# Two pairs' keys times values as one run of products, in front of their queries; whole transposes for the second batch; a new order of the opening

## The chip, the cores and the metric

The kernel runs on one core of one Trainium2 chip. The metric is the device time of one execution in microseconds (us); the smaller, the better. Before the change it is 903.7 us, the median of three runs (903.17 to 904.11).

## What is computed

An attention without softmax, then a feed-forward block:

```python
kv  = np.einsum('bhsd,bhse->bhde', k, v)      # 8 batches, 8 heads, 576 tokens, 64 features
out = np.einsum('bhsd,bhde->bhse', q, kv)
rms = np.sqrt(np.mean(out * out, axis=-1, keepdims=True) + 1e-06)
x   = out / rms * g_norm                      # heads side by side: 4608 tokens x 512
g   = np.maximum(x @ w_in, 0.0) ** 2          # w_in 512 x 2048, w_out 2048 x 512
y   = g @ w_out
```

Everything is computed in float32. The weights arrive as 64-bit floats, so the kernel loads them as raw words and converts them itself.

## The kernel before, in words

**Heads come in pairs.** Four pairs (p = 0 to 3) hold the eight heads of a batch b. A pair's 576 tokens are four chunks of 128 tokens and 64 last tokens. The last tokens of an even batch lie in partitions 0 to 63 of k_rest, v_rest and q_rest, those of the odd batch after it in partitions 64 to 127.

**Keys times values** (key_value, L399 to L430) takes for each pair, chunk and head a product of 128 tokens by 64x64 features, and at the end of the pair, for each head, one over the 64 last tokens. Each float32 product is two instructions in the trace. The first kind uses half the columns of the array (128*64 in the profile), the second a quarter of it (64*64). ACT then copies the sums into kv_all (L418, L419). key_value is called for one pair at a time in batches 0 and 1 and for two pairs from batch 2 on.

**Queries are transposed** in transposed_query (L365 to L393): for batches 0 and 1 on TensorE, by a product with an identity (L388), one for each chunk and head, so 16 instructions a pair. For later batches VectorE does it (L371). The queries' last tokens of both first batches go through nc.tensor.transpose (L396), four for all four pairs, which are four instructions.

**Queries times kv** (products_x, L432 to L451) makes two tiles of tokens (a pair of ns) from 64 instructions in the same 64*64 form as the last tokens' products. query (L486) issues products_x, then key_value for the next batch if it was given keys, and then the squares; query_means (L493) is the same without keys and with the means. The rest of the normalising is on VectorE (DVE), with the root on ACT.

**The feed-forward** works in nine strips of 512 tokens. Its matrices are multiplied by Strassen's scheme: seven products for eight. Strip 0 computes the up half plainly (up_first, L749) and the down half with one level (down), strip 1 has one level up (up) and two down (down_deep), the later strips two levels in both (up_slot, down_deep). The second level's weights are sums that strip 0 and 1 make on DVE and POOL, store in DRAM (w_out, w_deep, w_in_deep) and stream back (w_blk).

**The opening** (L639 to L647) is a list of slices: act (ACT's two passes over a weight piece, L241 and L244), piece (its four DVE steps, L253 to L262), T (transposed_query), K (key_value), Q (first_queries, L522, with its squares and means), N (first_normalized, L531), F (first_features, L546) and U (first_up, L556, the products of strip 0's first weight columns). Every engine runs its share of a slice in the order of the list, and waits in that order.

**After the opening** attend(n) issues slices up to number n between the steps of the strips. In strip 0, step i runs up_first for i below n_up = 16 and down afterwards; the slices of batch 1 are spread by L1261 to L1263. In strip 1 they are spread evenly over 25 steps.

**The order of transfers** is SP's: nearly all DMAs are issued by SP in program order, and SP waits in front of each for what it needs. The pairs of batch 1 are loaded by load_next in steps 0 and 1 of strip 0, except pair 3, whose load (k, v, then q) is issued inside key_value of pair 0 (load_next at the end of key_value). Batch 1's q comes with one DMA a pair, in packets of 1 KB.

Of the kernel before, what the change touches and what calls it, by code (L numbers as in the profile page):

```python
# [10 lines left out]
FP32 = mybir.dt.float32  # L11
# [9 lines left out]
def kernel(  # L21
# [34 lines left out]
    nc = tc.nc  # L56
    P = 128
    B, H, S, D = q.shape
# [3 lines left out]
    NP = H // 2  # L62
    FC = d_ff // P
    C = S // P
    REST = S - C * P
# [37 lines left out]
    def load(b, p, q_eng, names="kvq", parts=range(4)):  # L103
        hs = slice(2 * p, 2 * p + 2)
        inputs = (("q", q, q_eng), ("k", k, nc.sync), ("v", v, nc.sync))
        if b == 0 and p >= 2:

            h_place = g_pool.tile([P, 4, C * P], FP32, name="first_qkv", tag="gt")
        if b == 1 and p == 2:
            h_place = spare_pool.tile([P, 3, C * P], FP32, name="more_qkv")  # L110
        placed = (b, p) in ((0, 2), (0, 3), (1, 2))
        for i, (n, src, eng) in enumerate(inputs if b == 0 else inputs[1:] + inputs[:1]):
            if n not in names:
                continue
            whole = src[b, hs, 0 : C * P].rearrange("h (sp c) d -> sp h c d", c=C)
            if n == "q" and b >= Q_ON_PE:

                t = qkv_pool.tile([P, 4 * C, SQ], FP32, name=n, tag=n, bufs=3) if 0 in parts else main[n, b, p]
                for a in parts:
                    h, f = divmod(a * SQ, D)  # L120
                    eng.dma_start(
                        out=t[ts(a, SQ)],
                        in_=src[b, 2 * p + h, 0 : C * P, f : f + SQ].rearrange("(k i) f -> i k f", k=4 * C),
                    )
            elif n != "q":
                if placed:
                    t = h_place[:, i].rearrange("p (h c d) -> p h c d", h=2, c=C)
                else:
                    t = qkv_pool.tile([P, 2, C, D], FP32, name=n, tag=n)
                eng.dma_start(out=t, in_=whole)  # L130
            else:

                if placed:
                    t = h_place[:, i].rearrange("p (h c d) -> p h c d", h=2, c=C)
                else:
                    t = qkv_pool.tile([P, 2, C, D], FP32, name=n, tag=n, bufs=3)
                eng.dma_start(out=t, in_=whole)
            main[n, b, p] = t


# [218 lines left out]
    def keep_busy(ps, n):  # L359


        for _ in range(n):
            nc.tensor.matmul(ps, lhsT=ident, rhs=ident[:, : ps.shape[1]], start=True, stop=True)

    def transposed_query(b, p):  # L365
        while any(f == load and a[:2] == (b, p) for f, a in drips):
            drip()
        t = main.pop(("q", b, p))
        if b >= Q_ON_PE:
            qT[b, p] = qt_pool.tile([P, C, P], FP32, name="qT", tag="qT")  # L370
            nc.vector.transpose(out=flat(qT[b, p]), in_=flat(t))  # L371
            if b % 2 and p == NP - 1:
                while any(f == load_q_rest and a[0] <= b for f, a in (*rest_drips, *drips)):
                    drip(not drips)
                nc.vector.transpose(
                    out=open_rest(b).rearrange("p q (k t) -> p q k t", k=4),
                    in_=squares(q_rest[b // 2]).rearrange("p k q f -> p q k f"),
                )
            drip_queries()
            if p == NP - 1 and b + 1 < B:  # L380
                (rest_drips, drips)[b % 2 == 0].extend((load_q_rest, (b + 1, nc.sync, a)) for a in range(4))
            return
        ps = apsum.tile([P, C, P], FP32, name="t_ps", tag="at")
        if (b, p) == (0, 0):
            keep_busy(ps[:, 0], 7)
        for c in range(C):
            for h in range(2):
                nc.tensor.matmul(ps[ts(h, D), c, :], lhsT=t[:, h, c], rhs=ident, start=True, stop=True)  # L388
        qT[b, p] = qt_pool.tile([P, C, P], FP32, name="qT", tag="qT")
        nc.scalar.copy(qT[b, p], ps)  # L390
        if (b, p) == (1, NP - 1):
            drip_queries()
# [6 lines left out]
    def key_value(b, *ps_of):  # L399
        while any(f == load and a[:2] == (b, p) or f == load_rest and a[0] == b for _, f, a in keys_due for p in ps_of):  # L400
            _, f, a = keys_due.popleft()
            f(*a)
        ps = apsum.tile([P, len(ps_of), D], FP32, name="kv_ps", tag="at")
        for i, p in enumerate(ps_of):
            tk, tv = main.pop(("k", b, p)), main.pop(("v", b, p))
            if (b, p) == (0, 0):
                keep_busy(ps[:, 0], 5)
                warm = apsum.tile([P, NT, P], FP32, name="x_ps", tag="first")[:, 0]
            half = slice(REST * (b % 2), REST * (b % 2 + 1))
            for c in range(C + 1):  # L410
                if (b, p, c) == (0, 0, C):
                    keep_busy(warm, 2)
                for h in range(2):
                    a, w = (t[:, h, c, :] if c < C else r[half, 2 * p + h] for t, r in ((tk, k_rest), (tv, v_rest)))
                    nc.tensor.matmul(ps[ts(h, D), i], lhsT=a, rhs=w, start=c == 0, stop=c == C)  # L415
        at = (NP * b + ps_of[0]) % (2 * NP)
        d = kv_all[:, at : at + len(ps_of)]
        nc.scalar.copy(d[0:D, :, 0:D], ps[0:D])  # L418
        nc.scalar.copy(d[D:P, :, D:P], ps[D:P])  # L419
        for i, p in enumerate(ps_of):  # L420
            kvd[b, p] = d[:, i]
            if b < 2:
                if b == 1 and p == 0:
                    load_next()
            else:
                u = next(to_load, None)
                if u is not None:
                    keys_later(load, *u, nc.sync, "kv")
                if p == NP - 1 and b + 1 < B:
                    keys_later(load_rest, b + 1, nc.sync)  # L430
# [30 lines left out]
    def mean_of(sqs):  # L461
        ms = small.tile([P, 2, H], FP32, name="ms", tag="ms")[:, : len(sqs)]
        for i, sq in enumerate(sqs):
            if len(sq.shape) == 3:
                sq = sq.rearrange("p r e -> p (r e)")
            nc.vector.reduce_sum(out=ms[:, i], in_=by_head(sq), axis=AX.X)
        nc.vector.tensor_scalar(out=ms, in0=ms, scalar1=1.0 / D, scalar2=EPS, op0=ALU.mult, op1=ALU.add)
        return ms
# [15 lines left out]
    queried = []  # L484

    def query(ns, *keys):  # L486
        ps = products_x(ns)
        if keys:
            key_value(*keys)
        parts = [ps[:, :, i] for i in range(len(ns))]  # L490
        queried.append((parts, squared_parts(parts, c_pool, "c")))

    def query_means(ns):  # L493
        ps = products_x(ns)
        parts = [ps[:, :, i] for i in range(len(ns))]
        queried.append((parts, mean_of(squared_parts(parts))))

    def roots_normalized(ns):
        parts, ms = queried.pop()
# [123 lines left out]
        convert_on_act, transposed_query, key_value, first_queries, first_normalized, first_features, first_piece  # L623
    )
    U = first_up
    slices += [(T, (0, 0)), (K, (0, 0)), (T, (0, 1)), (Q, (0,)), (K, (0, 1)), (N, (0,)), (T, (0, 2)), (Q, (1,))]
    slices += [(act, (0,)), (F, (0,)), (K, (0, 2)), (piece, (0, 4)), (N, (1,)), (T, (0, 3)), (Q, (2,)), (act, (1,))]
    slices += [(F, (1,)), (U, (0, [0])), (K, (0, 3)), (piece, (1, 4)), (N, (2,)), (U, (0, [1])), (Q, (3,)), (act, (2,))]
    slices += [(F, (2,)), (U, (0, [2])), (piece, (2, 2)), (N, (3,)), (act, (3,)), (U, (1, [0])), (piece, (2, 2))]
    slices += [(F, (3,)), (piece, (3, 4))]  # L630
    slices += [(U, (1, [1, 2])), (U, (2, [0, 1, 2])), (U, (3, [0, 1, 2]))]
    ready[0] = len(slices)
    def query_pairs(b):
# [1 line left out]
        ns = list(range(first_n, first_n + C + b % 2))  # L635
        return [ns[i : i + 2] for i in range(0, len(ns), 2)]

    for p in range(NP):
        slices += [(transposed_query, (1, p)), (key_value, (1, p))]  # L639
    for pair in query_pairs(1)[1::-1]:  # L640
        slices += [(query_means, (pair,)), (roots_normalized, (pair,))]
        if pair == query_pairs(1)[1]:
# [1 line left out]
        slices += [(features, (n,)) for n in pair]  # L644
    ready[1] = len(slices)
    T, K, last = transposed_query, key_value, query_pairs(1)[2]
    slices += [(query_means, (last,)), (K, (2, 0, 1)), (T, (2, 0)), (roots_normalized, (last,)), (T, (2, 1))]  # L647
    slices += [(T, (2, 2)), (features, (last[0],)), (T, (2, 3)), (K, (2, 2, 3))]
    for b in range(2, B):
        pairs = query_pairs(b)  # L650
# [517 lines left out]
    for s in range(N_STRIP):  # L1168
# [23 lines left out]
        for i, (w, fn, a) in enumerate(steps):  # L1192
# [65 lines left out]
                sums_in((7, 8, 9, 12).index(i - n_up))  # L1258
            if i == n_up + 11:
                sums_x(1)  # L1260
            n = i + 1 - (n_up - 6)  # L1261
            pairs, m = divmod(max(n - 2 * NP, 0), 3)
            attend(min(ready[0] + min(max(n, 0), 2 * NP) + (n >= 2 * NP) + 4 * pairs + (0, 2, 2)[m], goal))  # L1263
            while deep_due and i != n_up + 1:
                store_deep_sums(*deep_due.popleft())
            if 11 <= i < n_up:
# [32 lines left out]
```

## Time and profile before

| | |
|---|---|
| Median of three runs | 903.7 us |
| The profiled execution's own time | 903.58 us |
| Its span in the profile | 901.6 us |
| Granted TensorE clock | 1.00 of full speed |
| TensorE busy | 886.6 us, 98% |
| VectorE busy | 734.4 us, 81% |
| ScalarE and GpSimd busy | 315.3 and 306.5 us |
| DMA | 235.73 MB, mean 261 GB/s |

The profile is of one execution. Times in it count from the start of its span. PE is TensorE, PEld its weight loads, DVE is VectorE, ACT ScalarE, POOL GpSimd, and SPq the queue of SyncE that issues the DMAs. A line of a timeline gives the start, the length, the engine, the line of the kernel, the operation with the tiles that it writes and reads, the shapes, and how many instructions are merged. A PE instruction's own length includes its latency; what a stream of them costs is the distance of their starts.

### The profile page before, as it was taken

The numbers are of one execution on the slowest core, as the hardware profiler recorded it, in microseconds if no ns is written. First come the engines' busy times: TensorE is split into PE (matmuls) and PEld (weight loads), VectorE is DVE, ScalarE is ACT, GpSimd is POOL, SyncE is SP. The second block draws the span as 40 slices with busy tenths as digits, with TensorE's granted clock in tenths as the row PEclk, the third lists the DMA queues.
The fourth block names the chain that finished last, engine by engine and source line by source line (L and its number), as shares of the span: only waits on it lengthen the run. The fifth ranks groups of instructions, "written<-read, shape, count | busy, mean of one in ns | idle before, by whom it ended". The sixth has DMA issues, their size and how long they took to land.

```text
span 901.6 us, 20778 instructions
## 1 busy us (share of the span) xinstructions
PE 886.6 (98%) x8348; PEld 826.8 (92%) x8348; DVE 734.4 (81%) x1256; ACT 315.3 (35%) x622; POOL 306.5 (34%) x315
## 2 busy tenths in 40 slices
PE   7999999999999999999999999999999999999998
PEld 6445888889999999999999999999999999999998
DVE  3899999769878986798689966986799778875886
ACT  4798241320027302640255023810272027102710
POOL 0000005700448223731374034704461446144700
PEclk9999999999999999999999999999999999999999
DMA  9998998999988798979787878798647865784385
GB/s 296 310 307 249 297 345 248 286 291 346 304 210 269 262 326 237 253 255 321 231 244 249 318 235 240 223 316 301 197 163 275 307 195 183 282 308 158 124 307 190
DMA packets 166096, 235.73 MB, mean 261 GB/s; under 512 B 75248, under 2 KB 131056, under 8 KB 157552
## 3 DMA queue, kind: packets, MB, share of 16 engines
q1 hardware_dynamic: 165840, 234.40, 80.4%
q8 instruction: 66, 1.08, 0.5%
q14 instruction: 30, 0.25, 0.1%
q10 hardware_dynamic: 160, 0.00, 0.0%
HBM read 197.66 MB, written 36.70 MB: 260 GB/s over the span
## 4 chain that ended last, share of the span: by engine, by line
PE 88%; DVE 5%; DMA 4%; issue 1%; SPq 1%; ACT 0%; DVEq 0%; ACTq 0%
PE ps_B L930 21%; PE ps_A L1118 17%; PE ps_A L930 17%; PE ps_B L1118 9%; PE ps_A L715 5%; PE ps_C L1118 4%; PE kv_ps L415 2%; PE ps_A L756 2%; PE ps_B L715 2%; PE x_ps L449 2%; PE ps_C L756 2%; PE ps_C L715 1%; PE ps_B L756 1%; DMA w_blk<-w_deep 1%; DVE gt L1130 1%
## 5 line engine op out<-in xcount | busy, mean ns | idle before, releaser
L930 PE MATMUL ps_B<-w_blk,g_s 128*128 128x128 f32 x1024 | 126.2, 275 | 0.0
L930 PEld LDWEIGHTS ps_B<-w_blk,g_s 128*128 128x128 f32 x1024 | 120.0, 192 | 0.2
L1118 PE MATMUL ps_A<-x_l,w_in 128*128 128x128 f32 x784 | 104.1, 276 | 0.0
L279 POOL TENSOR_TENSOR x_l<-xT 128x256 f32<-128x256 f32 x21 | 15.6, 741 | 248.1 <-PE ps_A L930 248.1
L930 PE MATMUL ps_B<-w_blk,gt 128*128 128x128 f32 x768 | 97.5, 275 | 0.3 <-DMA w_blk<-w_deep 0.3
L1118 PEld LDWEIGHTS ps_A<-x_l,w_in 128*128 128x128 f32 x784 | 95.4, 192 | 0.5 <-DVE gt L1130 0.2
L930 PE MATMUL ps_A<-w_blk,g_s 128*128 128x128 f32 x768 | 93.6, 275 | 0.0
L930 PEld LDWEIGHTS ps_B<-w_blk,gt 128*128 128x128 f32 x768 | 91.5, 192 | 0.5 <-DMA w_blk<-w_deep 0.5
L930 PEld LDWEIGHTS ps_A<-w_blk,g_s 128*128 128x128 f32 x768 | 89.6, 192 | 0.0
L1130 POOL TENSOR_TENSOR snap<-snap,gt 128x512 f32<-128x512 f32 x35 | 46.5, 1329 | 122.3 <-ACT snap L1135 55.2
L1135 ACT COPY snap<-ps_A 128x512 f32<-128x512 f32 x63 | 36.6, 582 | 132.5 <-PE ps_A L1118 119.2
L945 DVE TENSOR_TENSOR o_sb<-o_sb,ps_B 128x256 f32<-128x256 f32 (+1 forms) x128 | 49.5, 387 | 34.6 <-ACT o_sb L946 27.3
L1068 ACT ACTIVATE gt<-gt 128x512 f32<-128x512 f32 x112 | 69.7, 622 | 18.1 <-DVE gt L1130 18.0
L930 PE MATMUL ps_A<-w_blk,gt 128*128 128x128 f32 x576 | 72.2, 275 | 0.0
L1069 ACT ACTIVATE gt<-gt 128x512 f32<-128x512 f32 x112 | 70.6, 631 | 3.6
L930 PEld LDWEIGHTS ps_A<-w_blk,gt 128*128 128x128 f32 x576 | 68.2, 192 | 0.0
L1130 POOL TENSOR_TENSOR gt<-gt,snap 128x512 f32<-128x512 f32 x42 | 52.5, 1275 | 24.7 <-DVE snap L1130 24.7
L279 DVE TENSOR_TENSOR gt<-gt 128x2048 f32<-128x2048 f32 (+1 forms) x29 | 59.7, 2063 | 0.0
L1028 POOL TENSOR_TENSOR w_i<-w_in 128x512 f32<-128x512 f32 x7 | 9.2, 1314 | 143.5 <-DVE w_in L279 142.8
L946 ACT COPY o_sb<-ps_A 128x128 f32<-128x128 f32 x24 | 6.4, 265 | 145.8 <-PE ps_A L930 145.8
L1118 PE MATMUL ps_A<-x_l,w_blk 128*128 128x128 f32 x392 | 52.3, 276 | 1.4 <-issue 1.2
L1118 PE MATMUL ps_B<-x_l,w_blk 128*128 128x128 f32 x392 | 52.0, 276 | 0.0
(178 smaller groups left out, 1817.6 us busy)
## 6 DMA issues: line engine op xcount, KB each, us to landing
w_blk<-w_deep SPq DMA_DIRECT2D x56, 1024.0 KB, 6.5
w_blk<-w_out SPq DMA_DIRECT2D x56, 768.0 KB, 5.9
w_blk<-w_in_deep SPq DMA_DIRECT2D x49, 768.0 KB, 4.8
raw<-in_moe_w_in_dram SPq DMA_DIRECT2D x16, 512.0 KB, 7.6
raw<-in_moe_w_out_dram SPq DMA_DIRECT2D x16, 512.0 KB, 6.4
k<-in_k_dram SPq DMA_DIRECT2D x29, 256.0 KB, 4.9
v<-in_v_dram SPq DMA_DIRECT2D x29, 256.0 KB, 5.2
x_d<-x_q SPq DMA_DIRECT2D x27, 256.0 KB, 5.4
```

What stands on the lines that cost most here:

```text
L279: eng.tensor_tensor(out=out, in0=a, in1=b, op=ALU.subtract)
L415: nc.tensor.matmul(ps[ts(h, D), i], lhsT=a, rhs=w, start=c == 0, stop=c == C)
L449: nc.tensor.matmul(ps[half, r, i, ts(p, D)], lhsT=q[row, half], rhs=kvd[b, p][row, row], start=True, stop=True)
L715: nc.tensor.matmul(bank[BANK[p]][:, i, :], lhsT=lhsT(k), rhs=rhs(k), start=p in (1, 5, 2) and i == 0 and k == 0, stop=k == n - 1, skip_gro ...
L756: nc.tensor.matmul(ps, lhsT=w_in[:, kc % KH, g, kc // KH * 2 + fh, ts(i, P)], rhs=xt[0][:, :, kc, :], start=kc == 0, stop=kc == NP - 1,)
L930: nc.tensor.matmul(chain[c][x][:, i, :], lhsT=a[:, f, :], rhs=w[:, f, :], start=x not in opened[c] and f == 0, stop=f == FQ // 2 - 1, skip ...
L945: add = lambda out, a, b: nc.vector.tensor_tensor(out=out, in0=a, in1=b, op=ALU.add)
L1068: nc.scalar.activation(o, o, AF.Relu)
L1069: nc.scalar.activation(o, o, AF.Square)
L1118: nc.tensor.matmul(ps[:, i, :], lhsT=w, rhs=rhs, start=j in (1, 2, 5) and i == 0, stop=True, skip_group_check=True)
L1130: add = lambda eng, out, a, b: eng.tensor_tensor(out=out, in0=a, in1=b, op=ALU.add)
L1135: nc.scalar.copy(t, ps)
```

## The change

It has four parts.

1. key_value issues all chunks of its one or two pairs first and then the last tokens' products of these pairs. The start flag is set for the first chunk of the first pair only.
2. Batch 1 calls key_value for two pairs at a time, after the transposes of both. Its spread over strip 0's steps (L1261) changes with it: the first transpose comes one step later, at most one slice is issued a step for five steps, and the second two pairs' keys with the first queries at the place where the fourth pair's keys were. query issues key_value in front of products_x, and query_means can take keys, issued right behind its products and means. The keys of batch 2's first two pairs go there.
3. Batch 1's queries lie in SBUF with the two heads side by side (p, c, h, d), filled by one DMA for each head, and are transposed by nc.tensor.transpose, one for each chunk with both heads.
4. In the opening, each piece's ACT passes and its DVE steps stand earlier in the list: piece 0 ahead of the third transpose, piece 1 ahead of the fourth, piece 2 whole and ahead of the last queries.

```diff
-            else:
+            elif b == 0:
...
+            else:
+
+                if placed:
+                    t = h_place[:, i].rearrange("p (c h d) -> p c h d", h=2, c=C)
+                else:
+                    t = qkv_pool.tile([P, C, 2, D], FP32, name=n, tag=n, bufs=3)
+                for h in range(2):
+                    eng.dma_start(out=t[:, :, h, :], in_=whole[:, h])
@@ transposed_query
         for c in range(C):
+            if b:
+                nc.tensor.transpose(ps[:, c, :], flat(t[:, c]), ident)
+                continue
@@ key_value
-        for i, p in enumerate(ps_of):
-            tk, tv = main.pop(("k", b, p)), main.pop(("v", b, p))
...
-            for c in range(C + 1):
...
+        tiles = [[main.pop((n, b, p)) for n in "kv"] for p in ps_of]
+        steps = [(i, c) for i in range(len(ps_of)) for c in range(C)] + [(i, C) for i in range(len(ps_of))]
+        for i, c in steps:
...
+                nc.tensor.matmul(
+                    ps[ts(h, D), i], lhsT=a, rhs=w, start=i == 0 and c == 0, stop=c == C, skip_group_check=True
+                )
@@ query, query_means
     def query(ns, *keys):
-        ps = products_x(ns)
         if keys:
             key_value(*keys)
+        ps = products_x(ns)
...
-    def query_means(ns):
+    def query_means(ns, *keys):
...
+        if keys:
+            key_value(*keys)
@@ the opening
-    slices += [(T, (0, 0)), (K, (0, 0)), (T, (0, 1)), (Q, (0,)), (K, (0, 1)), (N, (0,)), (T, (0, 2)), (Q, (1,))]
-    slices += [(act, (0,)), (F, (0,)), (K, (0, 2)), (piece, (0, 4)), (N, (1,)), (T, (0, 3)), (Q, (2,)), (act, (1,))]
-    slices += [(F, (1,)), (U, (0, [0])), (K, (0, 3)), (piece, (1, 4)), (N, (2,)), (U, (0, [1])), (Q, (3,)), (act, (2,))]
-    slices += [(F, (2,)), (U, (0, [2])), (piece, (2, 2)), (N, (3,)), (act, (3,)), (U, (1, [0])), (piece, (2, 2))]
-    slices += [(F, (3,)), (piece, (3, 4))]
+    slices += [(T, (0, 0)), (K, (0, 0)), (T, (0, 1)), (Q, (0,)), (K, (0, 1)), (N, (0,)), (act, (0,)), (piece, (0, 4))]
+    slices += [(T, (0, 2)), (Q, (1,)), (F, (0,)), (K, (0, 2)), (N, (1,)), (act, (1,)), (U, (0, [0])), (piece, (1, 4))]
+    slices += [(T, (0, 3)), (Q, (2,)), (F, (1,)), (U, (0, [1])), (K, (0, 3)), (N, (2,)), (act, (2,)), (piece, (2, 4))]
+    slices += [(Q, (3,)), (U, (0, [2])), (F, (2,)), (U, (1, [0])), (N, (3,)), (act, (3,)), (F, (3,)), (piece, (3, 4))]
@@ batch 1, and the last pair of tiles before strip 2
-    for p in range(NP):
-        slices += [(transposed_query, (1, p)), (key_value, (1, p))]
+    for p in range(0, NP, 2):
+        slices += [(transposed_query, (1, p)), (transposed_query, (1, p + 1)), (key_value, (1, p, p + 1))]
...
-    slices += [(query_means, (last,)), (K, (2, 0, 1)), (T, (2, 0)), (roots_normalized, (last,)), (T, (2, 1))]
+    slices += [(query_means, (last, 2, 0, 1)), (T, (2, 0)), (roots_normalized, (last,)), (T, (2, 1))]
@@ strip 0's steps
-            n = i + 1 - (n_up - 6)
-            pairs, m = divmod(max(n - 2 * NP, 0), 3)
-            attend(min(ready[0] + min(max(n, 0), 2 * NP) + (n >= 2 * NP) + 4 * pairs + (0, 2, 2)[m], goal))
+            n = i + 1 - (n_up - 5)
+            pairs, m = divmod(max(n - 7, 0), 3)
+            attend(min(ready[0] + min(max(n, 0), 5) + 2 * (n >= 7) + 4 * pairs + (0, 2, 2)[m], goal))
```

More of the change, by code (lines that the diff above doesn't have):

```diff
@@ L403, in key_value @@
         ps = apsum.tile([P, len(ps_of), D], FP32, name="kv_ps", tag="at")
-        for i, p in enumerate(ps_of):
-            tk, tv = main.pop(("k", b, p)), main.pop(("v", b, p))
[L406 to L409, printed above, removed]
-            for c in range(C + 1):
[L411 to L415, printed above, removed]
+        if (b, ps_of[0]) == (0, 0):
+            keep_busy(ps[:, 0], 5)
+            warm = apsum.tile([P, NT, P], FP32, name="x_ps", tag="first")[:, 0]
+        half = slice(REST * (b % 2), REST * (b % 2 + 1))
+        tiles = [[main.pop((n, b, p)) for n in "kv"] for p in ps_of]
+        steps = [(i, c) for i in range(len(ps_of)) for c in range(C)] + [(i, C) for i in range(len(ps_of))]
+        for i, c in steps:
+            if (b, ps_of[i], c) == (0, 0, C):
+                keep_busy(warm, 2)
+            for h in range(2):
+                at = (slice(None), h, c) if c < C else (half, 2 * ps_of[i] + h)
+                a, w = (t[at] for t in (tiles[i] if c < C else (k_rest, v_rest)))
+                nc.tensor.matmul(
+                    ps[ts(h, D), i], lhsT=a, rhs=w, start=i == 0 and c == 0, stop=c == C, skip_group_check=True
+                )
         at = (NP * b + ps_of[0]) % (2 * NP)
```

## The prediction, put on record before the change ran

> **What bounds the kernel now.** I read the page first, then the busy times by stretch, PE's timeline, the waits of PE and of SP, and last the chain of waits. The page's first part:
>
> ```profile
> PE 886.6 (98%) x8348; PEld 826.8 (92%) x8348; DVE 734.4 (81%) x1256; ACT 315.3 (35%) x622; POOL 306.5 (34%) x315
> ```
>
> PE sets the time on average, with only 11 us of idle. But what a saved PE microsecond is worth differs by stage (stretch, then sum, PE, PEld, DVE, ACT, POOL, clock, DMA share, GB/s):
>
> ```profile
> 37.00:97.00 60.00, 60.00 (x267) 30.91 (x267) 58.90 (x135) 50.82 (x108) 0.00 (x0) 1.00 0.91 281
> 97.00:150.00 53.00, 53.00 (x420) 46.12 (x418) 51.68 (x85) 16.69 (x24) 4.79 (x3) 1.00 0.92 306
> 150.00:205.00 55.00, 54.77 (x476) 47.23 (x474) 41.12 (x66) 15.75 (x33) 24.48 (x18) 1.00 0.95 284
> 205.00:901.60 696.60, 688.83 (x6952) 681.34 (x6952) 561.54 (x921) 212.91 (x418) 275.62 (x287) 1.00 0.77 252
> ```
>
> Until 150 us DVE is as full as PE, until 205 us DMA is at 0.91 to 0.95; from 205 us on PE alone is full. How close the others are, PE's and SP's timelines tell: SP issues the weights of strip 0's product 3 at 119.92, its next DMA waits until they land, and PE begins the product at 129.95.
>
> ```profile
> 119.92 0.37 SPq L810 DMA_DIRECT2D w_blk<-w_out  x1
> ```
> ```profile
> SPq L121 <- DMA w_blk<-w_out: 3.2, 1, 3.2
> ```
> ```profile
> 129.95 7.07 PE L715 MATMUL ps_B<-w_blk,gt 128*128 128x256 f32 x32
> ```
>
> By its semaphore this DMA lands at 129.32: PE could not have come more than 0.6 us earlier. In the chain of waits the next place is 205:
>
> ```profile
> 189.85 6.57 DMA xT<-x_d
> 196.43 1.07 SPq L600
> 197.55 7.45 DMA w_blk<-w_deep
> 205.04 1.05 PE ps_B L930 x7
> ```
>
> Here PE already waits 0.3 us for w_blk, though busy by the page. The opening's own line among PE's waits, for the features' transposes, is DVE's:
>
> ```profile
> PE xt_ps L551 <- DVE x_n L534: 3.2, 3, 1.4
> ```
>
> **What the Trainium skill says.** "TensorEngine Tiling (Array Packing)", section Tiling Modes, Key Properties: a change of tiling mode drains TensorE. The trace agrees. Here are a query and its keys:
>
> ```profile
> 268.58 1.16 PE L449 MATMUL x_ps<-kv_all,qT 64*64 64x64 f32 x64
> 269.68 0.69 PE L415 MATMUL kv_ps<-v,k 128*64 128x64 f32 x16
> 270.29 0.33 PE L415 MATMUL kv_ps<-v_rest,k_rest 64*64 64x64 f32 x4
> 270.55 0.69 PE L415 MATMUL kv_ps<-v,k 128*64 128x64 f32 x16
> 271.17 0.33 PE L415 MATMUL kv_ps<-v_rest,k_rest 64*64 64x64 f32 x4
> 271.43 1.16 PE L1118 MATMUL ps_B<-x_t,w_blk 128*128 128x128 f32 x8
> ```
>
> By single starts two heads' instructions follow each other every 58 ns; where the form changes, the first comes 152 ns after the last (52 within a form) and the second 106 after the first: 148 ns a change, and about 200 ns back to the full array. "Perfetto Trace Analysis", section Optimizing Tensor Performance, Transposes: use a transpose, not a standard matmul. The trace agrees: L388 has 16 instructions for what L396 does in 4. "DMA: Bandwidth & Descriptors", section Why small descriptors are slow: each packet has a fixed overhead. In this trace packets of 256 B took 18 ns (median; mean 26), of 1 KB 46 (mean 53).
>
> **The change, part by part.**
>
> *Transposes of batch 1.* From the last full product before L388 to the first after it are 1.547 us, less the ordinary 0.429, plus 0.104 by which the second one is late: 1.22 us a pair. The four instructions of L396 cost 0.44 (653 + 110 ns less two starts of 0.216, and the chain has 0.44). So 4 x 0.78 = 3.1 us less of PE.
>
> *Keys in twos.* A call for two pairs spends 1605 ns from first to last start; with two changes of form less it is 1605 - 2 x 148 = 1309. 12 calls from batch 2 on: 0.296 us each. For batch 1 two single calls (1.074 each) become one of 1.66: 2 x 0.49 = 0.98 us.
>
> *Keys ahead of queries.* The last tokens' products run straight into the queries' in one form: one more change of 148 ns goes, less some 35 that mixing them cost at 97.4 us (1104 ns against 943 + 117). So 0.41 us for each of the nine calls in query. The call now behind query_means saves the way back to full and out again but for one change: 0.49 with its 0.296. The two calls alone save 0.29. Of these calls three lie before 205 us (0.49 + 0.29 + 0.41 = 1.2 us) and nine after it: 8 x 0.41 + 0.29 = 3.6 us. ACT's order does not change (copies of kv, then squares), and the squares come some 0.7 us sooner; k and v were there 2.5 us or more ahead of every call after 205. The last tokens are tighter: batch 4's land at 268.70 and would be used near 269.7, batch 7's at 556.54 and 556.7. Those loads follow PE's own releases, so I put them at nothing; uncovered, each costs up to 1 us, and the products behind it wait too. Below nothing: PE's waits for DVE in the up stages (2.9 us after 205, most of them behind queries) may shrink, because sums of squares stand earlier. I take 0.3, between 0 and 1.5.
>
> *The opening.* One file on DVE: a piece takes 2.36 us from the first step to the next instruction (0.46 + 0.46 + 0.84 + 0.6, rows of 16.3 to 25 us), a mean with its normalising 2.77 us to the end of x_n (0.72, 0.21 for the root, 0.24, 0.91, 0.69). Before, the means of query n stood in front of a piece; now behind it. Piece 0 can start at 14.60 (behind x_n of 0), so mean 1 at 16.97; then a round is 2.69 + 2.36 = 5.05: mean 2 at 22.02, mean 3 at 27.07, its x_n at 29.84 and the last F at 29.87. Before it was 29.72. ACT's passes fit: piece 0 landed at 12.24, and ACT is free at 13.05. So the opening ends 0.15 us later, not sooner, with PE idle in one block (26.1 to 29.9) in place of six. The bounds are 0.7 us sooner and 1.5 later, for hops of semaphores that I moved by rows, not by measurement. The bound on PE's clock is with the rivals.
>
> *Transfers.* Four more DMAs on SP (0.45 to 0.6 us of issue each) and 1024 packets of 256 B for 256 of 1 KB: by the rows above 0.4 to 0.9 us a pair of all engines' time, at a DMA share of 0.98 to 0.91. The pieces behind them come up to 2 us later; DVE takes pieces 16 and 17 some 1.6 us after ACT has them, and the queue empties once at 37 us: nothing, at worst 0.5. Pair 3's load now hangs on the joint key_value, two steps later, and behind SP's four stores of w_out (until 80.3): k, v and q land by 86 as I estimate from this trace's spacing of 0.7 us per 256 KB. PE wants that q at 84.9, so it waits about 1 us, and everything queued behind on PE waits with it. This costs nothing in the end: up to 92.8 it is covered by the wait that follows.
>
> *What is late next.* By 120 us PE would be 0.98 + 3.1 - 0.15 = 3.9 us ahead, less that wait. But product 3's weights are behind SP's order and a DVE without one idle gap above 0.3 us from 38.5 to 150; none of it is in the change. PE may gain 0.63 - 0.15 there and no more. At 148.5 the last tokens of batch 2 (landing 149.14) stop the joint call again, at 168 the queries' last pair waits for q that lands at 167.82 (DVE transposes it until 168.7, PE used it at once), and at 205 w_blk comes: 0.27 of waiting, and 0.33 of SP's wait for x_q at 182.3, are all that can be won. So of 5.3 us saved before 205 I count 0.3.
>
> *The sum*, against the profiled execution's 903.58 (span 901.6 and 1.98 around it): 903.58 - 0.3 - 3.6 - 0.3 = 899.4; the median of the runs stands 0.1 above this execution, so 899.5.
>
> **Rivals.**
>
> *All of it counts.* If the weights of product 3 and w_blk at 205 come sooner with PE, 3.1 + 0.98 + 1.2 + 3.6 - 0.15 = 8.7 us: 895.0. For it speaks PE's 98%; against it DVE's and DMA's columns above.
>
> *Little is left.* The later savings go into waits for last tokens and for DVE's sums, or the idle block before the last F costs clock: the first keep-busy products ran every 213 ns until 4.7 us and every 110 afterwards, so a cold PE runs at half speed for 3.4 us. "TensorE: Matmul & The Clock Gate", section Part 1, gives an idle window of about 3.4 us for falling back; my block is 3.7 us. It would cost 1.7 to 3.4 us at the start: 899.5 + 3.4 = 902.9.
>
> *Slower.* The opening, if ACT's two passes (1.25 us a piece) are not hidden any more, since they now stand ahead of the copies of the transposed queries: 3 x 1.25 more in the last F (33.6 us), an idle PE of 7 us, and with it surely the half clock (3.4): 7.2 later, all of it handed on by DVE's full stretch to 150. 899.5 + 7.2 = 906.7. For it: every engine waits in the list's order. Against it: pieces landed ahead of their use in my working. It decides when the first product of L756 begins more than 4.2 us after its 37.06.
>
> **How the numbers follow.** Main case 0.60 (898 to 901.5), all counts 0.13, little left 0.15, slower 0.12. A measurement of this kernel can tell about 0.2%, 1.8 us, from no change. Faster is the main case, the first rival and a fifth of the second: 0.76; the rest of the second is the same: 0.12; slower 0.12. The range goes from 895.0 to 902.9, from the one rival's time to the other's, and leaves out the slower case and half of the first rival.
>
> **What would show it.** Right: four transposes of 0.44 us in batch 1; 32 chunk instructions of keys, then 8, then queries without a gap; the last F near 29.9; PE idle for about 2 us before product 3 (near 129.4) and for over 0.3 us before 205; later stages ahead by 0.4 us per joint call. Wrong: PE at product 3 or at 205 us several us ahead of before, a granted clock below 1 near 30 us, or waits of PE for v_rest.

## The result

The kernel after takes 908.17 us, the median of five runs (906.98 to 909.18), against 903.7 before: a ratio of 1.0051, interval [1.0036, 1.0066]. It is slower, and 8.7 us above the forecast. The profiled execution took 908.17 us itself, its span is 905.0.

The first part of the page of after, engines and their shares:

```profile
PE 881.2 (97%) x8300; PEld 823.8 (91%) x8300; DVE 734.6 (81%) x1256; ACT 315.0 (35%) x618; POOL 306.3 (34%) x315
```

TensorE has 5.4 us less busy time than before, although a half clock stretches some of it (below), and the span is 3.4 us longer, so 8.8 us are new waiting. The busy times by stretch of after tell where (stretch, sum, PE, PEld, DVE, ACT, POOL, clock, DMA share, GB/s):

```profile
37.00:97.00 60.00, 58.58 (x227) 30.29 (x227) 55.85 (x127) 51.06 (x106) 0.00 (x0) 1.00 0.84 252
97.00:150.00 53.00, 48.99 (x366) 42.30 (x362) 49.73 (x89) 15.69 (x22) 0.00 (x0) 1.00 0.96 325
150.00:205.00 55.00, 52.01 (x487) 44.72 (x486) 40.55 (x60) 15.94 (x33) 28.82 (x21) 1.00 0.90 256
```

Before, PE had no gap from 37 to 150 us and DVE 2.4 us; now PE misses 5.4 us there and DVE 7.4, and PE 3.0 more up to 205 (before 0.2). By name, from PE's waits of after (us in total, times, longest):

```profile
PE xt_ps L567 <- DVE x_n L550: 3.5, 1, 3.5
PE ps_A L730 <- DMA w_blk<-w_out: 1.8, 1, 1.8
PE kv_ps L427 <- DMA v_rest<-in_v_dram: 1.8, 2, 1.5
...
PE ps_A L730 <- DVE gt L793: 1.5, 1, 1.5
PE t_ps L396 <- DMA q<-in_q_dram: 1.4, 1, 1.4
```

Three places stand in these lines: the opening (L567 is the last F), the transfers of strip 0 (w_blk, q), and the keys of batch 2 (v_rest, gt). The table shows when a kernel reaches the same product of the program, as the start in its trace less that of before (us; at the end, the end of the last product). Columns e5 to e15 are experiments that are described below.

| | start of before | after | e5 late load | e8 opening | e9 own slice | e15 |
|---|---|---|---|---|---|---|
| first product of strip 0's own steps | 37.06 | +2.43 | +0.58 | +2.68 | +0.97 | +0.01 |
| strip 0, product 6 | 115.09 | +2.18 | +0.58 | +2.68 | -1.18 | -2.96 |
| strip 0, product 3 | 129.95 | +4.77 | +3.43 | +2.68 | +1.82 | -0.88 |
| strip 1's down half | 201.93 | +6.61 | +3.39 | +2.69 | +1.08 | -1.34 |
| strip 2 | 243.56 | +7.07 | +2.85 | +2.16 | +1.39 | +0.25 |
| end | 897.62 | +3.29 | +2.96 | +3.79 | -2.69 | -3.82 |

So after loses 7.07 us by strip 2 and wins 3.78 back from there to the end. The chain of waits of after (start, length, what) no longer has the DMA that stood in it at 197 to 205 before; from v_rest on TensorE is on it, except from 160 to 164 us (ACT and DVE, up to gt):

```profile
151.68 3.64 DMA v_rest<-in_v_dram
155.45 0.45 PE kv_ps L427 x8
...
206.98 1.73 PE ps_A L730 x8
208.71 6.51 PE ps_B L945 x56
```

### The profile page after: what moved, and what is told of

The parts are those of the page before. It is cut to its first block, busy times and chain, and to the rows that moved or that the text cites. A ratio compares the mean times of both kernels' runs of the same rounds, so it can differ in the third digit from the quotient of the medians.

```text
span 905.0 us, 20689 instructions
## 1 busy us (share of the span) xinstructions
PE 881.2 (97%) x8300; PEld 823.8 (91%) x8300; DVE 734.6 (81%) x1256; ACT 315.0 (35%) x618; POOL 306.3 (34%) x315
## 4 chain that ended last, share of the span: by engine, by line
PE 72%; DMA 10%; DVE 9%; ACT 4%; issue 2%; SPq 2%; DVEq 0%; ACTq 0%
PE ps_B L945 21%; PE ps_A L945 16%; PE ps_A L1133 15%; PE ps_B L1133 8%; PE ps_C L1133 3%; PE ps_A L730 3%; DMA w_deep<-w_t 2%; PE kv_ps L427 1%; PE ps_B L730 1%; DMA v_rest<-in_v_dram 1%; ACT raw L252 1%; ACT w_c L249 1%; PE x_ps L463 1%; DVE gt L1145 1%; DMA w_blk<-w_deep 1%
```

## The experiments

Each was compared with the kernel before on its own chip, where that took 904.3 to 904.5 us (27 to 51 runs). Single executions of one kernel spread by up to 9 us there (e2), so a ratio is over many runs, and a profiled execution may lie off its median: a trace shows where time is lost in one execution, the ratios what a part costs.

**The opening.** e8_new_opening is the kernel before with the four new lines of the opening's list.

> The kernel before with the new order of the opening alone. The first product of strip 0's own steps comes 2.2 to 2.6 us later, half of it from the clock at 0.5. If DVE, full from there to 150 us, hands all of it on: 906 to 906.8 us. If stretches that wait for DMA take it up (strips 1 and 2): 904 to 905 us. My prediction gave the opening 0.15 us.

907.16 us, ratio 1.0024 [1.0016, 1.0032]. PE's timeline of e8, then a stretch of after with the clock:

```profile
30.71 0.63 PE L551 MATMUL xt_ps<-ident,x_n 128*128 128x128 f32 x4 [3.53 <-DVE x_n L534]
```
```profile
30.70:34.10 3.40, 3.40 (x8) 1.80 (x7) 2.53 (x5) 2.71 (x5) 0.00 (x0) 0.50 0.97 290
```

PE is idle 3.53 us in one block (3.54 in after), and the next 3.4 us run at clock 0.50 (the column in front of the DMA share). From the last F to the first product of strip 0's own steps it takes 9.01 to 9.03 us in all five traces of the new order without filling products, and 7.33 to 7.34 with the old: 1.69 us for the clock in these traces. The last F itself stands at 30.36 in the median of nine traces with the new order and at 29.76 in eight with the old: 0.6 more. In e8's trace the delay is handed on whole up to strip 1's down half.

e1_warm, e11_new_opening_warm and e13_new_opening_warm_twice fill the idle block with products by the identity whose result nobody reads (keep_busy):

```diff
@@ first_features, of after (e1), of e8 (e11), of e8 (e13)
+        if p == NP - 1:
+            keep_busy(ps[:, 0], 12)
@@ transposed_query, e13 alone
+        if (b, p) == (0, 2):
+            keep_busy(ps[:, 0], 4)
```

> The changed kernel with twelve idle products of the identity on TensorE (they fill nothing but time, into a tile that is overwritten) in the idle block ahead of the opening's last F. Theory (the half clock after a 3.5 us idle block costs 1.7 us, and DVE's full stretch hands it on): the granted clock stays at 1.00, the first product of strip 0's own steps begins near 37.7 instead of 39.48, and the time is 1.7 us shorter than the changed kernel's, about 906.4. Rival (the opening does not matter, the loss is made in the transfers after 80 us): clock 1.00 too, but the time stays at about 908.

> The kernel before with the new opening order (as e8_new_opening) and 12 products with the identity into the last F's PSUM tile ahead of its transposes, so that TensorE is not idle in one block. If half of the opening's loss is the clock, the first product comes at 37.4 to 37.8 and it takes 904.6 to 905.6 us. If it is VectorE's and ScalarE's later order alone, it stays at 906.5 to 907.

> The kernel before with the new opening, 12 filling products ahead of the last F as in e11_new_opening_warm, and 4 more ahead of the third pair's transposes. In e12_single_keys_warm TensorE was slow from 14 to 18 us behind a wait for that pair's query. If such a second slow window is what left e11_new_opening_warm at +1.9 us though its trace shows a first step on time, this run takes 904.3 to 905.3 us. If not, it stays at 906 to 907, and something other than the clock makes the typical execution late.

e1 takes 908.8 us (1.0045 [1.0031, 1.0059]), e11 906.38 (1.0024 [1.0013, 1.0034]), e13 906.87 (1.0025 [1.0017, 1.0034]). The products do their part in the traces: here e11 goes on at full speed.

```profile
26.24 2.94 PE L363 MATMUL xt_ps<-ident 128*128 128x128 f32 x24
29.77 0.65 PE L553 MATMUL xt_ps<-ident,x_n 128*128 128x128 f32 x4 [0.59 <-DVE x_n L534]
30.27 1.02 PE L564 MATMUL ps_B<-xT,w_in 128*128 128x512 f32 x2
```

But the time does not follow. In e1 the 2.0 us are gone again at product 3 of strip 0 (+3.51) and at strip 1's down half (+6.41 against 6.61 in after), in waits for w_blk (1.98 and 1.82) and v_rest (2.05): there the transfers set the pace. In e11's profiled execution (903.52, the shortest of its sixteen) the gain holds to the end (-0.08), and in e13's the loss is +0.66 at the first product and +1.52 at the end; their medians stay 1.9 and 2.5 above before.

The mean granted clock of each execution tells how far this is the clock's doing. In e8 it is 0.995 to 0.998 in all 22 executions; one window of 3.4 us at half the clock lowers the mean of an execution to 0.998. In e11 it is 0.999 or 1.000 in 14 of 16, in e13 in 21 of 22. So the clock came back there in nearly every execution and the time did not, and a second slow window, e13's question, is not the reason. What costs these two kernels 2 us is then the new order with the clock whole; the products are not what the last F waits for in e11's trace, since it still stands 0.59 us for x_n behind them. How the order does it in the typical execution stays open, and the 1.69 us of the traces are not shown in any median. e1 tests this less well: only its profiled execution has 1.000, the other four 0.996 to 0.998.

**Pair 3's load.** e5_late_load issues it in before where after does:

```diff
-                if b == 1 and p == 0:
+                if b == 1 and p == 1:
                     load_next()
```

> The kernel before, with pair 3's load of batch 1 issued two steps later (after the second call of key_value instead of the first) and nothing else. If the load's new place in SP's order is a cost by itself, the raw pieces 28 and 29 land some 6 us later, the stores of w_out and PE's weight blocks with them, and the run takes 905 to 906.5 us. If it costs only together with a DVE that is late from the opening, PE's slack of 0.6 us before product 3 is lost and little more: 904 to 904.5 us. My prediction priced it at nothing, at worst 0.5.

906.66 us, ratio 1.0022 [1.0013, 1.0032]: a cost by itself, and more than the 0.6 us of slack of the second guess. SP's timeline of before, then of e5:

```profile
70.00 0.37 SPq L130 DMA_DIRECT2D k<-in_k_dram  x1
70.42 0.46 SPq L130 DMA_DIRECT2D v<-in_v_dram  x1
70.93 0.47 SPq L137 DMA_DIRECT2D q<-in_q_dram  x1
...
81.68 0.89 SPq L229 DMA_DIRECT2D raw<-in_moe_w_out_dram  x2
```
```profile
81.00 0.52 SPq L130 DMA_DIRECT2D k<-in_k_dram  x1
81.56 0.56 SPq L130 DMA_DIRECT2D v<-in_v_dram  x1
82.17 0.47 SPq L137 DMA_DIRECT2D q<-in_q_dram  x1
82.75 0.92 SPq L229 DMA_DIRECT2D raw<-in_moe_w_out_dram  x2
```

The pieces are issued only 1.07 us later (0.58 of it from this execution's opening), but the first lands at 89.44 for 86.33, and the stores behind it keep most of this lag: the last one that the first weight block waits for lands at 107.15 for 104.57. Product 3's own weight block lands at 133.24 for 129.32. PE's timeline of e5 at product 3:

```profile
133.38 0.89 PE L715 MATMUL ps_B<-w_blk,gt 128*128 128x256 f32 x3 [2.60 <-DMA w_blk<-w_out]
```

768 KB have moved from a stretch with room to 81 us and later, in front of a stretch that was full already. The busy times of before around both places, then of after:

```profile
70.00:76.00 6.00, 6.00 (x31) 3.05 (x32) 6.00 (x13) 5.87 (x16) 0.00 (x0) 1.00 0.75 228
...
84.00:90.00 6.00, 6.00 (x37) 3.52 (x36) 6.00 (x16) 4.32 (x10) 0.00 (x0) 1.00 1.08 334
90.00:100.00 10.00, 10.00 (x133) 8.33 (x132) 10.00 (x24) 3.11 (x9) 0.00 (x0) 1.00 1.10 320
```
```profile
70.00:76.00 6.00, 6.00 (x22) 3.04 (x21) 6.00 (x15) 5.78 (x14) 0.00 (x0) 1.00 0.37 130
```

"DMA: Bandwidth & Descriptors", section Issuing engines are not separate DMA queues, says that DMAs run on the same 16 engines and interleave, whichever engine issued them. Here 768 KB in front cost the first piece 2.5 us and the last store 2.0, when the 0.58 of this execution's opening is taken off; three times the 0.7 us per 256 KB of the prediction makes 2.1. The figure that would have priced the lag stood in the prediction.

e6_single_keys puts batch 1's slices and spread back into after:

```diff
-    for p in range(0, NP, 2):
-        slices += [(transposed_query, (1, p)), (transposed_query, (1, p + 1)), (key_value, (1, p, p + 1))]
+    for p in range(NP):
+        slices += [(transposed_query, (1, p)), (key_value, (1, p))]
...
-            n = i + 1 - (n_up - 5)
+            n = i + 1 - (n_up - 6)
...
```

> The kernel after, with batch 1's keys one pair at a time and its old spread over strip 0's steps, so that pair 3's load goes back to its old place; all else as after. If the load behind the joint call is the second cause, the raw pieces land near 87 us again, the waits for w_blk at products 6 and 7 go and it takes 905 to 906.5 us. If the opening alone holds the loss, it stays within 1 us of after (907.5 to 909).

905.06 us, ratio 0.9998 [0.9986, 1.001]. Against after this gains 4.8 us (1.0051 less 0.9998), more than the load costs alone. That the delays of opening and load add up in front of the same stores would explain it, which is argued and not shown: e6 takes the joint keys and their spread back as well, and its trace, of its longest execution (907.1), is level with after's at 140 us of before's time and at the end. e12_single_keys_warm adds e1's twelve products to it.

> The kernel after with batch 1's keys one pair at a time (as e6_single_keys) and the same 12 products. In e1_warm the clock came back and the time did not improve; if the late load behind the joint keys took that gain, it shows here: 902.8 to 904 us, over 1 us below e6_single_keys. If strip 1's transfers take it up instead, it stays at 905.

906.83 us, 1.0032 [1.0018, 1.0047]: no gain but a loss, against the first theory. In its trace PE ran at clock 0.55 from 15 to 18 us behind a wait of 2.2 us for the third pair's query, and the mean clock is 0.998 or less in 8 of its 11 executions, so the products did not keep the clock here. What made its runs long is not shown.

e7_raws_first keeps the joint keys in after and issues the load behind the two pieces:

```diff
                 if b == 1 and p == 0:
-                    load_next()
+                    pass
@@ strip 0's step, behind convert
+            if i == 13:
+                load_next()
```

> The kernel after, with joint keys kept, and pair 3's load issued behind raw pieces 28 and 29 of the same step instead of in front of them. If the order in SP's queue is what delays ACT, DVE and the stores, it gains 1.5 to 2.5 us on after (905.7 to 906.7), though PE waits for that pair's query some 1 us longer. If the late opening sets the time to 135 us anyway, it stays at 908.

911.59 us, 1.0076 [1.0054, 1.0098]: a miss. The load now waits in SP's queue behind stores that wait for DVE, and PE stands still for the pair's query (PE's timeline of e7):

```profile
95.78 0.44 PE L396 MATMUL t_ps<-ident,q 128*128 128x128 f32 x1 [8.35 <-DMA q<-in_q_dram]
```

**The keys inside query_means.** e2_old_opening is after with the opening's old list.

> The changed kernel with the opening's list as before; all else changed. Theory (of the loss up to 205 us, 2.4 us is the opening: 0.7 its later last F, 1.7 the half clock): first product of strip 0's own steps at 37.06 again, clock 1.00, about 905.7, so still slower than before, by the load of pair 3 and the waits behind it. Rival (the opening is the whole loss): about 899.9, the 3.8 us of later savings showing in full.

905.79 us, 1.0013 [0.9998, 1.0029], as the first theory expected in time; its profiled execution took 901.59, the shortest of its 14. e9_own_slice changes one more line of it:

```diff
-    slices += [(query_means, (last, 2, 0, 1)), (T, (2, 0)), (roots_normalized, (last,)), (T, (2, 1))]
+    slices += [(query_means, (last,)), (K, (2, 0, 1)), (T, (2, 0)), (roots_normalized, (last,)), (T, (2, 1))]
```

> The kernel after with the old opening, and the keys of batch 2's first two pairs in a slice of their own behind query_means, as before. The parts measured singly (later keys -4.1, late load +2.0, transposes 0) would make -2.1 against before, but the kernel after with the old opening stood at +1.2. If the keys inside query_means are the missing 3 us, this run takes 901.5 to 903 us and the wait for v_rest at 150 us shrinks below 0.6. If the joint keys of batch 1 hold it, it stays at 905 to 906.

900.98 us, 0.9968 [0.9955, 0.998]: 4.1 us from this line alone (1.0013 less 0.9968). So most of what e2 was still losing is this line and not pair 3's load, to which the first theory had put it. PE's timeline of e2, then of e9, at these keys:

```profile
147.92 1.15 PE L427 MATMUL kv_ps<-v,k 128*64 128x64 f32 x32
150.60 0.45 PE L427 MATMUL kv_ps<-v_rest,k_rest 64*64 64x64 f32 x8 [1.53 <-DMA v_rest<-in_v_dram]
```
```profile
149.20 0.69 PE L463 MATMUL x_ps<-kv_all,qT 64*64 64x64 f32 x32
149.83 1.99 PE L731 MATMUL ps_A<-x_t,w_in 128*128 128x256 f32 x8
151.75 0.45 PE L427 MATMUL kv_ps<-v,k 128*64 128x64 f32 x8
```

With a slice of their own a product of strip 1 stands between queries and keys, and the last tokens are there in time. Later e2 waits again, for gt:

```profile
159.33 1.99 PE L731 MATMUL ps_A<-x_t,w_in 128*128 128x256 f32 x8 [1.18 <-DVE gt L794]
```

Between the products that before reaches at 140 and 160 us, e2's trace loses 3.0 us and e9's wins 0.3. after and e14 (below), the same pair with the new opening, show 3.3 lost and 0.3 won. So the loss arises here. e10_means_keys adds the keys inside query_means to e3 (below).

> The kernel before with the later joint keys (as in e3_later_keys) and also the keys of batch 2's first two pairs inside query_means; batch 1, transposes and opening as before. If these keys come too early for their last tokens and push what is behind them in strip 1: 901.5 to 903.5 us, over 1.5 above e3_later_keys, with a wait for v_rest of over 1 us near 149. My prediction gives 0.5 us of gain: 899.7.

902.61 us, 0.9986 [0.9976, 0.9995], 2.8 above e3. Its v_rest waits only 0.35 us; PE's timeline of e10 shows a second cost:

```profile
149.25 0.45 PE L416 MATMUL kv_ps<-v_rest,k_rest 64*64 64x64 f32 x8 [0.35 <-DMA v_rest<-in_v_dram]
157.65 1.99 PE L720 MATMUL ps_A<-x_t,w_in 128*128 128x256 f32 x8 [0.85 <-DVE gt L783]
```

One slice less in the list brings roots_normalized a place forward. In e10 DVE makes x_n at 156.31 and only then gt at 156.92; in e3 gt comes first, at 154.65, and x_n at 158.73. PE waits for gt. In after the same wait is 1.5 us. e10's trace, of its shortest execution (900.35), makes these delays up by the end; the typical execution, by the ratios, does not.

**The parts that were right.** e3_later_keys is before with the new key_value and with key_value ahead of products_x in query; e4_whole_transposes is before with the third part alone.

```diff
@@ query, e3 (with key_value as in the change)
-        ps = products_x(ns)
         if keys:
             key_value(*keys)
+        ps = products_x(ns)
@@ transposed_query, e4 (with the load as in the change)
+            if b:
+                nc.tensor.transpose(ps[:, c, :], flat(t[:, c]), ident)
+                continue
```

> The kernel before with two things of the change only: in calls of key_value for two pairs (batch 2 on) the chunks stand together and the last tokens' products behind them, and query issues the keys in front of its products. Batch 1, the means of the last pair before strip 2 and the opening as before. Theory (what is saved after 205 us counts, what is saved before does not): eight calls of 0.41 and one of 0.29 us, 3.6 us: about 900.1. Rival (the later savings go into waits for last tokens and for DVE's sums): 903 to 904.

> The kernel before with the whole transposes of batch 1 alone (queries with the heads side by side, two DMAs a pair in packets of 256 B, four transposes instead of sixteen instructions). Theory (PE's 3.1 us before 92 us vanish in the wait for product 3's weights, whose slack is 0.6): 903.1 to 903.7, with a wait of PE for w_blk of about 2.5 us near 129. Rival (the small packets crowd the pieces' transfers and hold up DVE): 905 or more, DVE idle between 40 and 97 us. Second rival (PE's 98% is what counts): 900.6.

e3: 900.2 us, 0.9955 [0.9939, 0.997]. e4: 903.99, 0.9998 [0.9987, 1.0009]; PE is 2.75 us ahead at product 6 and gives it back in waits for x_n (0.97), w_blk (0.67), v_rest (0.53) and qT (0.68) up to 170 us.

**Do the prices hold together?** From after, e14_after_own_slice takes back the line of query_means alone; e9 then also the opening; e15_single_own_slice then also batch 1's slices, so that the load is early. e15 is before with e3's and e4's edits.

> The kernel after, opening and all, with the keys of batch 2's first two pairs back in a slice of their own. If these keys cost about 3 to 4 us wherever they are, it takes 904 to 905.3 us, and the rest of the loss against e9_own_slice (3 us) is the opening's. If the late opening hides the wait for v_rest, it stays at 907 or more.

> The kernel before with the later joint keys and the whole transposes, everything else as before: e9_own_slice with batch 1's keys one pair at a time, so that pair 3's load is early. If the late load costs 2 us beside the other parts as it does alone, it takes 899 to 900 us, over 0.7 below e9_own_slice. If the whole transposes' gain covers it, the two agree within 0.5.

| | median | ratio to before | step |
|---|---|---|---|
| after | 908.17 | 1.0051 [1.0036, 1.0066] | |
| e14: batch 2's keys in their own slice | 904.83 | 1.0004 [0.9994, 1.0014] | -4.2 us |
| e9: and the old opening | 900.98 | 0.9968 [0.9955, 0.998] | -3.3 us |
| e15: and batch 1 one pair at a time | 899.79 | 0.9949 [0.9936, 0.9963] | -1.7 us |

A step is the difference of the ratios times 904. e15 beats both kernels and e3 is level with it: the whole transposes bring nothing that can be measured. The prices depend on the order in which they are taken, since e6 has the opening and the keys and stands only 4.4 above e15.

e16_later_keys_warm puts `keep_busy(ps[:, 0], 4)` ahead of the third pair's transposes and of each later F of e3.

> The best so far, e3_later_keys (900.2), with 4 filling products ahead of the third pair's transposes and of each later F, where TensorE is idle 0.5 to 1.5 us in its trace. If the clock falls in the opening of some executions, the median comes down to 899.3 to 900 and the spread is smaller; if not, it stays at 900.2, or the products delay a transpose by up to 0.5 us each (901).

900.89 us, 0.9966 [0.995, 0.9982]: no better than e3, which had a mean clock of 0.999 or 1.000 in five of six executions already. Filling products brought no measurable gain in any of the five kernels that have them; only in e11 and e13 did they bring back a clock that was missing in most executions.

## Why the prediction was wrong

Three terms of the sum failed. In the order of the last table, the call behind query_means was to save 0.49 us of PE's time and costs 4.2, the opening was to cost 0.15 and costs 3.3, and pair 3's load was to cost nothing, at worst 0.5, and costs 1.7 (taken back with batch 1's joint keys). That is 9.2 us, where the forecast was missed by 8.7; e15, without the three, takes 899.79 for the forecast of 899.5. Two of the signs that the prediction named for being wrong came: a clock below 1 near 30 us and waits of PE for v_rest.

**Transposes of batch 1: right.** Four instructions cost 0.43 us (70.39 to 70.82 in after) where I had 0.44, and by e4 none of the 3.1 us reaches the end, as counted.

**Keys in twos and ahead of queries: right after 205.** Batch 1's joint call takes 1.46 us (78.22 to 79.68) for my 1.66. From strip 2 to the end after wins 3.78 us where I had 3.6 + 0.3, and e3 4.1 over all.

**The call behind query_means: wrong, in sign.** I gave it 0.49 us of PE's own time. It costs 2.8 (e10 over e3) to 4.2 (after over e14). I had the number that speaks against it: the last tokens land at 149.14, and I wrote that they "stop the joint call again". I did not see that the call comes a product earlier, so that the wait grows (1.5 us in after), nor that a slice less in the list puts the normalising ahead of gt on DVE.

**The opening: the chain right, its price wrong.** I worked out 15.24 us from the start of piece 0 (14.60) to the end of the last x_n (29.84); eight of the nine traces with the new order show 15.3, after from 14.98 to 30.32. What failed is its base, taken from one execution: piece 0 starts between 14.38 and 15.24 in these traces, and the last F is 0.6 us later in the median, not 0.15. And the half clock, which I saw coming from a block of 3.7 us, stood with a rival at 0.15 though it comes in every trace of the new order without filling products. "TensorE: Matmul & The Clock Gate", Part 1, which the prediction names, gives an idle window of about 3.4 us; 3.53 us of idling brought the half clock in five traces of five, but here shorter blocks brought it too (last section). Measured, the opening costs 2.2 alone and 3.3 in company, and e11 and e13 say that most of the 2.2 stays without the half clock. So neither the 0.6 us nor the 1.69 explains the price of the typical execution.

**Transfers: "nothing, at worst 0.5" was wrong.** For pair 3's load I looked at who waits for pair 3's own data (about 1 us for q: right, 1.42 measured, though q landed at 88.5 and not by 86) and not at what lands behind it. In after ACT waits for the first piece behind it from 86.3 on:

```profile
92.87 0.68 ACT L249 ACTIVATE w_c<-raw 128x512 f32<-128x512 f32 x1 [6.59 <-DMA raw<-in_moe_w_out_dram]
```

In before the same wait was 1.61 us:

```profile
86.41 0.68 ACT L241 ACTIVATE w_c<-raw 128x512 f32<-128x512 f32 x1 [1.61 <-DMA raw<-in_moe_w_out_dram]
```

In after DVE gets its gap of 0.93 us at 95.02, and stores and weight blocks follow 6 us late (the last store lands at 110.61 for 104.57). Alone the late load costs 2.0 us (e5), at the end of the chain 1.7; beside the new opening and the early keys, taken back with the joint keys of batch 1, 4.8 (e6).

**Before 205: half right.** Of 5.3 us saved I counted 0.3, and e4 agrees for the 3.1 us of the transposes. But the slack of 0.6 us in front of product 3 has a second meaning that I left out: a stage where gains are not passed on can pass delays on almost whole. In the traces e5's 3.43 us at product 3 and e8's 2.68 from the opening are still 2.96 and 3.79 at the end.

**The rivals.** The slower one asked for the first product of strip 0 to be over 4.2 us late; it was 2.43, so that mechanism did not decide, and that its 906.7 us came nearest is luck. "Little is left" named two things that came, the half clock and the waits for last tokens, but the waits as lost gains and not as new delays, and the clock's price shows in no median.

**Open:** why the medians keep the opening's loss when the clock is restored, and why the load and the opening cost more in company than alone.

## What to carry to other kernels

In a stage where another resource ends the wait, price a change by what it delays there, not by what it saves: here gains vanished and most delays stayed. When a call is moved, follow every transfer issued inside it and ask what lands behind it, and whether the old place had room on the DMA engines that the new one lacks. In an order written out as a list, a slice that is taken out moves all the others forward on every engine.

## What the hardware showed

An idle block of 3.53 us in PE was followed by a stretch of 3.4 us at half the clock in each of the five traces that have it (0.50 from 30.7 to 34.1 in after), which took 1.69 us more. Shorter blocks did so too. In e12 the clock fell after 2.24 us of waiting and one us of work; here are PE's timeline and the stretch:

```profile
14.24 1.09 PE L399 MATMUL t_ps<-ident,first_qkv 128*64 128x128 f32 x16 [2.24 <-DMA first_qkv<-in_q_dram]
```
```profile
15.30:18.70 3.40, 3.40 (x24) 3.07 (x24) 2.13 (x4) 1.65 (x3) 0.00 (x0) 0.50 1.07 388
```

In e6 it fell during a wait of 2.69 us for w_blk (first line), while e5 kept it behind one of 2.60 (second line):

```profile
132.70:136.10 3.40, 2.77 (x7) 2.27 (x8) 3.37 (x7) 0.00 (x0) 0.00 (x0) 0.50 1.04 368
```
```profile
133.30:137.00 3.70, 3.62 (x17) 3.24 (x18) 3.63 (x7) 0.00 (x0) 0.00 (x0) 1.00 1.02 398
```

No block of up to 2.05 us (e1) brought it from 7 us on in these traces. So here the length of one block does not decide between 2.2 and 2.7 us, and 3.4 us of idling is no safe bound. The row of 40 slices on the profile page shows 9 throughout for after; the mean granted clock of the execution (0.998) and a stretch cut to 3.4 us show the fall.
